# A mixture-of-experts dispatch on one core: block loads cut to 256 KB, and a replicated maximum as four column tiles

## The chip, the cores and the metric

The kernel runs on one core of a Trainium2 chip. A core has five engines that run side by side: TensorE (PE, with its weight loads listed apart as PEld), VectorE (DVE), ScalarE (ACT), GpSimd (POOL) and SyncE (SP), which here issues nearly all transfers. Transfers run on the core's 16 DMA engines. The metric is the time of one execution on the device, in microseconds; smaller is better.

## The reference

```python
def _attn_ref(x, v, pos_emb, w1, w2):            # x, v: (4, 11456, 128)
    h_filt = (np.maximum(pos_emb @ w1, 0.0) @ w2) * np.exp(-0.01 * pos)[:, None]
    u = x * v
    y = causal long convolution of u with h_filt along the sequence (by FFT)
    return x * y

def _moe_ref(x, phi, w1, w2):                    # x: (45824, 128), 8 experts, 4 slots each
    logits = x @ phi                             # (45824, 32)
    d = softmax over the tokens of logits        # dispatch
    slot_input = d.T @ x                         # (32, 128)
    slot_out = per expert: relu(slot_input @ w1[e]) @ w2[e]      # hidden width 1024
    c = softmax over the slots of logits         # combine
    return c @ slot_out

reference = _moe_ref(_attn_ref(...).reshape(45824, 128), ...)
```

The result of the first function (the gated convolution) is the token matrix of the second. Everything is float32.

## The kernel before

**Convolution, 0 to about 720 us.** Eight groups of 16 channels go through a transform of four steps, p1 to p4, and a gate with x. Steps of neighbouring groups are interleaved by a written list. The gated result goes to a scratch in DRAM, `scr`, in 16 pieces (lines 456 to 471); each holds 128 rows (channels) of up to 3,296 tokens. The last group's gates are done in `last_gate`, seven in a row (t = 0 to 6); between them the first loads of the next stage are issued by `Moe.ahead`.

**Dispatch, about 730 to 817 us.** The 45,824 tokens are 23 blocks of 2,048 (the last of 768). `Moe.load(i)` brings block i from the scratch as 128 channels by 2,048 tokens: 1 MB in rows of 8 KB, one transfer for each piece of the scratch that the block touches. Blocks 0 to 4 are loaded in two parts: 112 channels ahead of the last group's gates (`Moe.weights`), the last 16 channels behind them. Blocks 5 to 9 are loaded by `ahead`, blocks 10 to 22 by `fetch(i)`, which is called behind the transposes of block i and loads into the place that falls free there: blocks 10 to 19 behind 0 to 9, then W1 of the experts (512 KB each, `load_w1`, two each behind blocks 10 to 13), W2 of three experts behind block 14, blocks 20 to 22 behind blocks 15 to 17, and the remaining W2 (`load_w2`). All of this stands on SP's queue in this order. The transfers use eight landing semaphores in turn, so SP issues one only when the one eight before it has landed.

Two blocks are a unit; there are 12 units, the last with one block. For unit m+1 PE computes the logits (`logits`, line 780: four products of 32 output partitions for a block, with 512 tokens each, which together read the whole block), and for unit m it transposes the tokens (`turn`, line 714) and multiplies them by the dispatch weights (`dispatch`, line 872: 32 products with 32 columns of weights). VectorE takes a unit's maximum for each slot; `running_max` spreads it over the partitions by a product with `reps` (a 32 by 32 identity repeated 4 by 4), and VectorE reduces the result to the new negative running maximum, which the exponentials (`exps`, ACT) take as their bias. The program's order on each engine is fixed by hand (`inorder`). In a round of the loop PE does: transposes of the unit's first block, logits of the next unit, transposes of the second block, dispatch products of the unit before, the product of `running_max`. A float32 product appears in the profile as two, each with its weight load: `running_max` as two records, a block's logits as eight, a full unit's 32 dispatch products as 64.

**Experts and output, 817 to 890 us.** Two layers for 32 slots, then 23 output tiles: product, copy, store.

Of the kernel before, what the change touches and what calls it, by code (L numbers as in the profile page):

```python
# [17 lines left out]
B, S, D = 4, 11456, 128  # L18
# [27 lines left out]
FF = 1024  # L46
# [592 lines left out]
class Moe:  # L639
# [3 lines left out]
    XB = 5  # L643
    OB = 4
    CB = 8 * NB

    def __init__(self, tc, cp, scr, phi, mw1, mw2, rep, out):
        self.tc, self.cp, self.scr, self.out = tc, cp, scr, out
        self.phi, self.mw1, self.mw2, self.rep = phi, mw1, mw2, rep

        self.blocks = [(q, min(self.NB, QN - q)) for q in range(0, QN, self.NB)]
        self.xt, self.xq = {}, {}
        self.pieces = sorted(_pieces().values())
# [14 lines left out]
            self.load(i, 0, D - CG)  # L668

    def load_w1(self, e):  # L670
        self.tc.nc.sync.dma_start(out=self.w1t[:, e], in_=self.mw1[e])

    def load_w2(self, e):
        self.tc.nc.sync.dma_start(out=self.w2t[e],
                                  in_=self.mw2[e])

    def logit_banks(self):
        self.pls = self.ctx.enter_context(ExitStack())
# [3 lines left out]
    def places(self):  # L682
# [4 lines left out]
        bufs = [self.xreg[:, i * sz : (i + 1) * sz] for i in range(n)]  # L687
        far = [self.E[:, self.CB * NSLOT + i * sz :][:, :sz] for i in range(2)]
        self.xbuf = bufs[: self.XB - 1] + far[:1]
        self.obuf = bufs[self.XB - 1 :] + far[1:]  # L690

    def load(self, i, d0=0, d1=D):
        q0, n = self.blocks[i]
        t = (self.ahead_buf if i // self.XB in (0, 2) else self.xbuf)[i % self.XB][:, : 128 * n]
        z0, z1 = 128 * q0, 128 * (q0 + n)
        for a, m in self.pieces:
            lo, hi = max(z0, a), min(z1, a + B * m)
            if lo < hi:
                src = self.scr[D * a : D * (a + B * m)].rearrange("(d t) -> d t", d=D)
                self.tc.nc.sync.dma_start(out=t[d0:d1, lo - z0 : hi - z0], in_=src[d0:d1, lo - a : hi - a])  # L700
        self.xt[i] = t.rearrange("p (q t) -> p q t", t=128)

    def turn(self, pool, tag, i, k0, k1, shared=False):
# [28 lines left out]
def _moe(mo):  # L732
    tc, cp, out, blocks, ctx = mo.tc, mo.cp, mo.out, mo.blocks, mo.ctx
    nc = tc.nc
# [4 lines left out]
    phis, reps, w1t, w2t = mo.phis, mo.reps, mo.w1t, mo.w2t  # L739

    inorder = tc.keep_in_program_order
    units = [(v, v + 1) for v in range(0, NBL - 1, 2)] + [(NBL - 1,)]
    NU = len(units)
    ereg = mo.E
    far = mo.CB * NSLOT + 4 * FF
    Cms = [ereg[:, : mo.CB * NSLOT], ereg[:, far : far + (QN - mo.CB) * NSLOT]]
    Cms = [c.rearrange("p (q s) -> p q s", s=NSLOT) for c in Cms]
    csum = ereg[:, QN * NSLOT + 4 * FF :][:, :QN]

    def weights_of(q0, n):  # L750
        assert (q0 < mo.CB) == (q0 + n <= mo.CB)
        return Cms[0][:, q0 : q0 + n] if q0 < mo.CB else Cms[1][:, q0 - mo.CB : q0 - mo.CB + n]

# [37 lines left out]
    def maxima(m):  # L791

        mask = pmt[:, 8:12] if m else mo.mask
        if m:
            lts[m] = ms.tile([128, 2 * NB, NSLOT], F32, tag="lt", name=f"lt_{m}", bufs=1)
            rd = ms.tile([128, 2, 4], F32, tag="rd", name=f"rd_{m}")
            rms = [ms.tile([128, 1], F32, tag=f"rm{k}", name=f"rm_{i}") for k, i in enumerate(units[m])]
        else:
            lts[m] = lt0
            rd = few[3][:, :8].rearrange("p (k a) -> p k a", k=2)  # L800
            rms = [few[4][:, k : k + 1] for k in range(2)]
        for k, i in enumerate(units[m]):
            inorder(nc.vector.tensor_reduce(out=rms[k], in_=pls[i].rearrange("p q t -> p (q t)"),
                                            axis=AX.X, op=ALU.max, negate=True))
            inorder(nc.vector.scalar_tensor_tensor(out=rd[:, k], in0=neg[:, m : m + 1].to_broadcast([128, 4]),
                                                   scalar=rms[k], in1=mask, op0=ALU.min, op1=ALU.mult))
            if m and k == 0 and m < last:
                scores(m, 0)
        return rd[:, : len(units[m])]

    def spread_max(m):
        rd = maxima(m)
        if m < last:
            scores(m, 1)
        return rd

    def running_max(m, rd, pm=None):
        if pm is None:
            pm = pmt[:, : 4 * len(units[m])]
        inorder(nc.tensor.matmul(pm, lhsT=reps, rhs=rd.rearrange("p k a -> p (k a)"), start=True, stop=True))  # L820
        inorder(nc.vector.tensor_reduce(out=neg[:, m + 1 : m + 2], in_=pm, axis=AX.X, op=ALU.min))

    def factor(m):
# [128 lines left out]
    def fetch(i):  # L952
        if i < 2 * XB:
            mo.load(i + 2 * XB)
        elif i < 2 * XB + 4:
            for e in range(2 * (i - 2 * XB), 2 * (i - 2 * XB) + 2):
                mo.load_w1(e)
        elif i < 3 * XB:
            for e in range(3):
                mo.load_w2(e)  # L960
        elif i + XB < NBL:
            mo.load(i + XB)
        else:
            for e in range(3 + 2 * (i + XB - NBL), min(NEXP, 5 + 2 * (i + XB - NBL))):
                load_w2(e, i)
# [9 lines left out]
    rd = maxima(0)  # L975
    for k in range(2):
        scores(0, k)
    yield
    running_max(0, rd, mo.spot)
    exps(0)  # L980
    yield
# [12 lines left out]
    rd = spread_max(1)  # L994
    turn(1)
    fetch(1)
    pas[0] = pp.tile([128, 128], F32, tag="pa", name="pa_0")
    warm(4)
    running_max(1, rd)
    factor(0)  # L1000
    for m in range(1, last - 1):
        u = units[m]
        exps(m)
        if m > LATE:
            invert_unit(m - LATE - 1)
        softmax(m)
        if m > LATE:
            scale_unit(m - LATE - 1)
        turn(u[0])
        fetch(u[0])  # L1010
        turn_weights(m)
        if m > 1:
            collect(m - 2)
        logits(m + 1)
        rd = spread_max(m + 1)
        if m == 2:
            softmax(0)
        elif 2 < m <= LATE + 2:
            norm(m - 3)
        turn(u[1])  # L1020
        fetch(u[1])
        dispatch(m - 1)
        running_max(m + 1, rd)
        factor(m)
    m = last - 1
# [9 lines left out]
    rd = spread_max(last)  # L1035
# [260 lines left out]
```

## Time and profile before

| what | value |
|---|---|
| median of 3 runs | 889.4 us (888.58 to 891.3) |
| profiled execution | 892.43 us, of which the span 890.7 us |
| mean granted TensorE clock | 0.992 |
| busy: PE, PEld | 857.9 us (96%), 791.0 us (89%) |
| busy: DVE, ACT, POOL | 714.5 us (80%), 455.1 us (51%), 393.1 us (44%) |
| moved by DMA | 197.02 MB, 94,386 packets, mean 221 GB/s |

The span runs from the first to the last instruction of the program; times in rows count from its start. Busy times are unions over an engine's instructions. A busy PE isn't PE at its peak, since the ends of its pipelined products are modelled. "Idle before" is the time in which an engine had nothing before an instruction, with what released it; "issue" means that nothing the profile shows released it.

### The profile page before, as it was taken

Reading aid. Unit: us, or ns where it says so; the run is one execution under the profiler, and the core shown is the slowest. Engines: PE = TensorE matmul, PEld = TensorE weight load, DVE = VectorE, ACT = ScalarE, POOL = GpSimd, SP = SyncE. Lnnn points to the kernel's source line nnn. Section 1 sums busy time; section 2 is a strip of 40 time slices with the busy share of each in tenths; the row PEclk is TensorE's granted clock in tenths of the full one; section 3 lists DMA queues with packets and bytes.
Section 4 is the critical chain, followed back from the end, with each engine's and each line's share of the span. In section 5 each row is a group of like instructions: output and inputs, shape, how many; then the busy total and the mean of one; then the engine's idle time right before and its main releaser. Section 6 shows DMA issues by size and latency. Waiting matters only on the chain. (4 is left out here: it accounts for less than half of the span.)

```text
span 890.7 us, 37282 instructions
## 1 busy us (share of the span) xinstructions
PE 857.9 (96%) x16192; PEld 791.0 (89%) x16192; DVE 714.5 (80%) x1239; ACT 455.1 (51%) x971; POOL 393.1 (44%) x538
## 2 busy tenths in 40 slices
PE   9999999999999999999999999999999999899991
PEld 8998989999999999999999999999999987566540
DVE  5967976799799889988988998899789058786791
ACT  5775558315811851472166128415811637887761
POOL 5003860492088019405910960393078013775750
PEclk9999999999999999999999999999999999999996
DMA  9963684457747754775486376557716979993698
GB/s 323 396 197 117 204 246 153 144 155 254 207 135 207 234 166 128 237 237 172 132 261 202 120 222 214 168 166 247 218 44 173 272 176 374 412 355 121 277 416 365
DMA packets 94386, 197.02 MB, mean 221 GB/s; under 512 B 14329, under 2 KB 55707, under 8 KB 90382
## 3 DMA queue, kind: packets, MB, share of 16 engines
q1 hardware_dynamic: 94046, 194.50, 67.0%
q8 instruction: 128, 2.10, 0.9%
q14 instruction: 36, 0.29, 0.1%
q10 hardware_dynamic: 144, 0.07, 0.0%
q0 software_dynamic: 32, 0.07, 0.0%
HBM read 137.73 MB, written 56.86 MB: 218 GB/s over the span
## 5 line engine op out<-in xcount | busy, mean ns | idle before, releaser
L350 POOL TENSOR_TENSOR T<-m 111x256 f32<-111x256 f32 (+1 forms) x199 | 150.9, 758 | 344.8 <-DVE m L344 344.8
L344 DVE TENSOR_TENSOR m<-p,T 111x1024 f32<-111x1024 f32 (+1 forms) x175 | 200.4, 1205 | 14.4 <-PE p L340 7.6
L360 PE MATMUL p<-tab,T 111*99 111x112 f32 x2048 | 205.4, 260 | 1.4 <-POOL T L351 0.3
L360 PEld LDWEIGHTS p<-tab,T 111*99 111x99 f32 x2048 | 198.8, 170 | 6.5 <-issue 1.6
L340 PE MATMUL p<-T,W 128*64 128x128 f32 (+1 forms) x3168 | 197.3, 276 | 0.4 <-issue 0.3
L425 ACT ACTIVATE vc<-p 128x412 f32<-128x412 f32 (+1 forms) x112 | 51.7, 513 | 266.4 <-PE p L412 227.0
L340 PEld LDWEIGHTS p<-T,W 128*64 128x64 f32 (+1 forms) x3168 | 182.0, 127 | 2.8 <-DVE m L344 0.6
L412 PE MATMUL p<-tab,E 99*64 99x103 f32 (+1 forms) x3584 | 174.0, 252 | 1.6 <-DVE E L373 0.6
L412 PEld LDWEIGHTS p<-tab,E 99*64 99x64 f32 x3584 | 166.2, 136 | 3.8 <-ACT vc L425 0.8
L375 ACT ACTIVATE E<-p 99x448 f32<-99x448 f32 x254 | 131.9, 575 | 63.9 <-PE p L360 57.8
L351 POOL TENSOR_TENSOR T<-m 111x256 f32<-111x256 f32 (+1 forms) x199 | 147.4, 741 | 0.0
L186 ACT ACTIVATE T<-p 128x396 f32<-128x396 f32 x240 | 100.2, 535 | 11.3 <-PE p L174 11.1
L174 PE MATMUL p<-tab1x,x 53*64 53x99 f32 x3648 | 86.7, 246 | 0.2 <-ACT E L224 0.2
L174 PEld LDWEIGHTS p<-tab1x,x 53*64 53x64 f32 x3648 | 79.8, 132 | 4.4 <-ACT E L224 0.4
L443 DVE TENSOR_TENSOR p<-p,vc 128x824 f32<-128x824 f32 (+1 forms) x46 | 47.0, 1022 | 8.9 <-ACT vc L425 8.9
L268 DVE TENSOR_TENSOR x<-x,T 128x448 f32<-128x448 f32 x51 | 31.6, 619 | 21.2 <-DMA x<-in_xf_dram 11.6
L274 DVE TENSOR_TENSOR x<-T 128x224 f32<-128x224 f32 x102 | 39.2, 426 | 1.8
L270 DVE TENSOR_TENSOR T<-x 128x224 f32<-128x224 f32 x102 | 39.2, 426 | 1.7
L224 ACT ACTIVATE E<-fl 111x512 f32<-111x512 f32 (+1 forms) x50 | 26.8, 627 | 21.3 <-PE fl L218 21.3
L451 DVE TENSOR_TENSOR E<-p,E 128x824 f32<-128x824 f32 x36 | 36.6, 1017 | 1.2
L720 ACT ACTIVATE xreg<-pt 128x512 f32<-128x512 f32 (+1 forms) x68 | 35.0, 609 | 1.0 <-PE pt L714 0.9
L344 DVE TENSOR_TENSOR m<-p,E 111x1024 f32<-111x1024 f32 (+1 forms) x25 | 28.7, 1201 | 5.1 <-PE p L340 4.9
(156 smaller groups left out, 972.1 us busy)
## 6 DMA issues: line engine op xcount, KB each, us to landing
x<-in_xf_dram SPq DMA_DIRECT2D x114, 256.0 KB, 4.2
out_dram<-xreg SPq DMA_DIRECT2D x16, 1024.0 KB, 10.6
E<-in_xi_dram SPq DMA_DIRECT2D x37, 412.0 KB, 3.9
T<-in_vf_dram SPq DMA_DIRECT2D x65, 224.0 KB, 5.1
scr<-E SPq DMA_DIRECT2D x67, 206.0 KB, 4.3
T<-hs SPq DMA_DIRECT2D x63, 154.0 KB, 4.5
hs<-E SPq DMA_DIRECT2D x12, 784.0 KB, 4.6
mv<-in_vf_dram SPq DMA_DIRECT2D x42, 224.0 KB, 4.6
```

The lines of the kernel that those rows point to most:

```text
L174: inorder(nc.tensor.matmul(ps[h][RP * d : RP * d + RP, i, s, :], lhsT=sd[js, i, s, d, :], rhs=tab1x[js, J * (s + d) : J * (s + d + 1)], st ...
L186: inorder(nc.scalar.activation(dst, src, AF.Copy))
L270: inorder(eng.tensor_tensor(out=vt[:, :, m : m + 2], in0=xr[:, :, 0:2], in1=xr[:, :, 2:4], op=op))
L340: inorder(nc.tensor.matmul(ps[ns, i].rearrange("p b c -> p (b c)"), lhsT=W[:, k0 + i, ns], rhs=Tf[:, :, k0 + i, :], start=True, stop=True, ...
L344: inorder(nc.vector.tensor_mul(m[:, :n].rearrange("p k s e c i -> p k s (e c i)").rearrange("p k s (b c) -> p k s b c", c=CG), ps[:, :n].u ...
L350: inorder(eng.tensor_tensor(out=Ty[:, 0], in0=m[:, :n, 0, 0], in1=m[:, :n, 1, 1], op=ALU.subtract))
L351: inorder(eng.tensor_tensor(out=Ty[:, 1], in0=m[:, :n, 1, 0], in1=m[:, :n, 0, 1], op=ALU.add))
L360: inorder(nc.tensor.matmul(pk[:, i, 2 * s : 2 * s + 2, :].rearrange("p q r -> p (q r)"), lhsT=T[0:N1, s, 2 * k + i, u // 2, :, u % 2], rhs ...
L375: inorder(nc.scalar.activation(dst, src, AF.Copy))
L412: inorder(nc.tensor.matmul(pv[RP * h : RP * h + RP, 2 * k + i, w, j0:], lhsT=E[:J, r, 2 - 2 * w + s, :], rhs=tab4[:, s, o + j0 : o + NJ], ...
L425: inorder(nc.scalar.activation(vc[:, w, :, j0:], pv[:, :, 0, j0:], AF.Copy, scale=2.0 * w - 1.0))
L443: inorder(nc.vector.tensor_tensor(out=pw[:, :, :, j0:], in1=vc[:, :, :, j0:], op=ALU.add, in0=pw[:, 1:2, :, j0:].to_broadcast([128, 2, 4, ...
```

## The change

Loads of blocks (where they begin at channel 0), of W1 and of W2 are cut into transfers of at most 512 tokens or columns, which is 2 KB a row. The loads of the last 16 channels of blocks 0 to 4 stay whole. The product of `running_max` becomes four products, each for 32 of the 128 output partitions, at column positions 0, 32, 64 and 96 of the array, as the logits and the dispatch products are placed.

```diff
+    RUN = 512
...
     def load_w1(self, e):
-        self.tc.nc.sync.dma_start(out=self.w1t[:, e], in_=self.mw1[e])
+        for f in range(0, FF, self.RUN):
+            self.tc.nc.sync.dma_start(out=self.w1t[:, e, f : f + self.RUN], in_=self.mw1[e, :, f : f + self.RUN])
 
     def load_w2(self, e):
-        self.tc.nc.sync.dma_start(out=self.w2t[e],
-                                  in_=self.mw2[e])
+        n = self.RUN // 128
+        for j in range(0, FF // 128, n):
+            self.tc.nc.sync.dma_start(out=self.w2t[e][:, j : j + n], in_=self.mw2[e, :, j : j + n])
...
         for a, m in self.pieces:
-            lo, hi = max(z0, a), min(z1, a + B * m)
-            if lo < hi:
-                src = self.scr[D * a : D * (a + B * m)].rearrange("(d t) -> d t", d=D)
+            lo, end = max(z0, a), min(z1, a + B * m)
+            src = self.scr[D * a : D * (a + B * m)].rearrange("(d t) -> d t", d=D)
+            while lo < end:
+                hi = min(end, z0 + ((lo - z0) // self.RUN + 1) * self.RUN) if d0 == 0 else end
                 self.tc.nc.sync.dma_start(out=t[d0:d1, lo - z0 : hi - z0], in_=src[d0:d1, lo - a : hi - a])
+                lo = hi
...
-        inorder(nc.tensor.matmul(pm, lhsT=reps, rhs=rd.rearrange("p k a -> p (k a)"), start=True, stop=True))
+        for a in range(4):
+            ss = slice(32 * a, 32 * a + 32)
+            inorder(nc.tensor.matmul(pm[ss], lhsT=reps[:, ss], rhs=rd.rearrange("p k a -> p (k a)"),
+                                     start=True, stop=True, tile_position=(0, 32 * a)))
```

## Rows read from the trace of the kernel before

**Rows 1.** Windows, dispatch: stretch, length, busy by engine (instructions), PE clock, DMA share, GB/s.

```profile
756.10:763.30 7.20, 6.72 (x149) 4.71 (x148) 6.27 (x11) 6.32 (x14) 5.62 (x4) 1.00 1.02 417
763.30:770.80 7.50, 6.61 (x149) 4.48 (x148) 5.63 (x10) 6.74 (x15) 5.58 (x8) 1.00 1.02 412
770.80:778.30 7.50, 6.55 (x147) 4.63 (x146) 5.72 (x10) 6.59 (x14) 4.93 (x6) 1.00 1.01 408
778.30:786.90 8.60, 6.87 (x149) 4.66 (x148) 6.04 (x12) 6.48 (x14) 6.96 (x9) 1.00 1.03 409
786.90:793.60 6.70, 6.70 (x149) 4.71 (x148) 6.03 (x12) 6.34 (x14) 5.26 (x6) 1.00 0.99 365
793.60:800.60 7.00, 7.00 (x148) 4.80 (x148) 6.14 (x12) 5.78 (x14) 6.01 (x8) 1.00 0.91 332
```

**Rows 2.** Timeline of PE, dispatch: start, length, line, operation, count, idle time before.

```profile
758.69 1.04 PE L780 MATMUL pl<-E,aux 128*32 128x512 f32 x8
...
772.61 0.58 PE L714 MATMUL pt<-aux,ffw 64*128 64x64 f32 x11 [0.95 <-issue]
...
779.29 1.15 PE L714 MATMUL pt<-aux,ffw 64*128 64x64 f32 x30 [0.70 <-issue]
...
786.00 0.64 PE L872 MATMUL pa<-E,ev 128*32 128x128 f32 x15 [1.03 <-issue]
```

**Rows 3.** The chain that ended last, dispatch: start, length, what.

```profile
766.07 0.36 issue
...
791.43 1.91 PE pa L872 x64
793.33 0.32 PE pmt L820 x2
...
798.12 2.23 PE pa L872 x64
...
801.80 1.92 PE pl L780 x16
...
814.13 0.62 issue
```

**Rows 4.** Timeline of PE around 70 us, in the convolution's first step.

```profile
69.88 2.97 PE L174 MATMUL p<-tab1x,mv 53*64 53x99 f32 x127 [0.47 <-issue]
74.12 1.60 PE L174 MATMUL p<-tab1x,mv 53*64 53x99 f32 x63 [1.27 <-issue]
```

**Rows 5.** Windows, early stretches of the kernel.

```profile
24.00:44.00 20.00, 19.40 (x239) 19.09 (x237) 19.31 (x52) 14.72 (x29) 0.00 (x0) 1.00 1.04 395
...
70.00:75.00 5.00, 3.73 (x168) 3.53 (x172) 2.33 (x5) 2.01 (x4) 0.00 (x0) 1.00 0.27 100
12.00:20.00 8.00, 7.83 (x68) 7.31 (x67) 6.60 (x16) 3.68 (x9) 0.40 (x2) 1.00 1.05 372
```

**Rows 6.** The page: busy times (instructions), and the instruction queue (packets, MB, share).

```profile
PE 857.9 (96%) x16192; PEld 791.0 (89%) x16192; DVE 714.5 (80%) x1239; ACT 455.1 (51%) x971; POOL 393.1 (44%) x538
...
q8 instruction: 128, 2.10, 0.9%
```

**Rows 7.** DMA issues at 794.6 to 795.2 us: count, KB, us to landing.

```profile
xreg<-scr SPq DMA_DIRECT2D x1, 1024.0 KB, 6.7
```

**Rows 8.** SP's waits from 690 us on: us in total, times, longest.

```profile
SPq L465 <- DVE aux L726: 14.7, 1, 14.7
...
SPq L700 <- DMA ffw<-scr: 8.7, 7, 2.0
```

**Rows 9.** DMA issues from 12 to 20 us.

```profile
W<-in_wt_dram SPq DMA_DIRECT2D x3, 499.5 KB, 6.3
T<-in_vf_dram SPq DMA_DIRECT2D x5, 224.0 KB, 5.1
E<-in_xf_dram SPq DMA_DIRECT2D x4, 256.0 KB, 5.1
```

**Rows 10.** SP's issues of line 700: ns of one, least, median and most.

```profile
L700 SPq DMA_DIRECT2D ffw<-scr x24: 303/443/979, 685.1 to 757.2; - x24
```

## The prediction

> **What bounds the kernel now.** I read the busy times by stage first, then the timeline of TensorE, then the chain that ended last, and last the DMA answers. In the dispatch, 756 to 800 us, PE is busy for 6.55 to 7.00 us of every unit of two blocks, and the units that last longer than 7 us are longer by idle time, not by work; the DMA share is 0.91 to 1.03 in the same rows, so two resources are nearly full at once [rows 1]. The output stage behind it multiplies by what the dispatch summed up, so neither its products nor its stores can begin earlier: every microsecond won or lost in the dispatch arrives at the end.
>
> What idles PE: the timeline shows pauses of 0.95, 0.70 and 1.03 us that nothing in the program releases ("issue"), in the middle of whatever line was running [rows 2]. Counted in that timeline, 127 products lie from 772.61 to 779.29 (six rows, the first of them here) and 127 more from there to 786.00 (six rows again). 127 products with their 127 weight loads are 254 instructions, and the page counts 128 transfers of 2.10 MB of instructions, 16 KB each, while PE executes 2 x 16,192 instructions: 253 for each transfer [rows 6]. So I read the pauses as PE waiting for its next 16 KB of program. From one resumption to the next it is 6.68 and 6.71 us [rows 2]. At 70 us, with the same spacing of 127 products, it is 4.24 us [rows 4], and there the DMA share was 0.27 [rows 5]. Loaded DMA engines thus cost an instruction fetch 2.45 us. The chain has three more such pieces: 0.36 us at 766, 0.62 us at 814, and a group of 64 products at 798 us that took 2.23 us where the one before took 1.91, so 0.32 [rows 3].
>
> **The loads in 2 KB rows: what it does to the fetch.** A block's load is 1 MB in 128 rows of 8 KB, 64 KB for each of 16 engines; at 410 GB/s over 16 that is 2.5 us, nearly exactly the 2.45 us. My reading is that the fetch waits behind what one load has put on its engine. Cut to 256 KB this is 0.64 us, and the period becomes 4.24 + 0.64 = 4.9 us. Its bounds are 4.24 (idle DMA) and 6.7 (as now). PE needs 5.7 us for its 127 products (6.68 - 0.95), so at 4.9 no pause is left. Up to block 21's logits that takes away 0.36 + 0.95 + 0.70 + 1.03 + 0.32 = 3.36 us, behind it 0.62.
>
> **What it does to the transfers.** A whole block becomes four transfers, five where a piece of the scratch ends inside it; a W1 or W2 load becomes two. On SP's queue an issue takes 0.44 us [rows 10]. Of blocks 0 to 4, 15 more issues (some 7 us) lie ahead of a wait of 14.7 us of SP for VectorE [rows 8], which hides them; without that cover they would delay the write of the first gated piece. Blocks 5 to 9 add 15 issues among the last gates' writes, where SP already waits for landings. Behind SP's waits stand the later gates' writes and the last input load; PE first uses block 9 at 758.7 us. I cost this by bandwidth below, not by issues, since 256 KB per 0.44 us is more than the engines move.
>
> Bandwidth is the price. Early in the kernel the DMA engines were also full (share 1.04 and 1.05), with transfers near the new size: 372 GB/s from 12 to 20 us, where twelve issues average 304 KB, nine of them 224 or 256 KB [rows 9], and 395 GB/s from 24 to 44 us [rows 5], against some 410 in the middle of the dispatch [rows 1]. So the new rate has bounds of 372 and 395 from rows, and 410 if smaller rows cost nothing. I take the middle of the two, 384.
>
> Who needs that bandwidth: blocks 20 and 21. Their buffers come free late (block 21's load is issued at 794.8 us and lands 6.7 us later, at 801.5 [rows 7]), and the logits of block 21 start at 801.80 + 0.96 = 802.76 us [rows 3]. That is a margin of 1.3 us, while PE without its pauses would be there 3.36 us earlier, and ten units' shorter maximum products (below) 0.8 earlier still: at 798.6. All else that SP queues goes ahead of block 21. From 756.1 to 800.6 us the windows moved 7.2 x 417 + 7.5 x 412 + 7.5 x 408 + 8.6 x 409 + 6.7 x 365 + 7.0 x 332 = 17.44 MB [rows 1]; less block 22 (0.39 MB), 17.05. The last two windows are below 410 because SP then waited for buffers; a PE that is ahead frees them earlier, so I let the new kernel run at its full rate to the end. At 384 GB/s the 17.05 MB take 44.4 us; blocks 5 to 9 (5.24 MB) are late by 5.24/0.384 - 5.24/0.410 = 0.9; landing follows the last byte by 1.0 (801.5 against 800.6). Block 21 is there at 756.1 + 0.9 + 44.4 + 1.0 = 802.4 us: 0.4 us before it is used now, 3.8 after PE would want it. By 395 it is 800.8 (2.0 earlier than now), by 372 it is 804.2 (1.4 later).
>
> The Trainium skill speaks against this part: DMA: Bandwidth & Descriptors, Rules for kernel authors, asks for 1 MiB or more per DMA for the most bandwidth. Its fit for one transfer, 2.0 us + bytes/436,000, gives 2.6 us for 256 KB, an estimate of 101 GB/s if they went one at a time. The rows above are of eight in flight, and show a loss of 4 to 9%, not of three quarters.
>
> **The running maximum's product.** Now it is two passes of one 128-column product, 0.32 us of the chain in each of 12 units [rows 3]. After, it is eight passes of 32 columns, of the same tile shape as the dispatch products that stand ahead of it. 64 of those take 1.91 us [rows 3], 0.030 each, so 0.24 us: 0.08 saved. Bounds: nothing saved (the change of shape only moves from before the product to after it) and 0.20 (four tiles side by side cost as one, 0.12). I take 0.08: 0.8 us before block 21's logits, 0.16 behind. VectorE's reduction waits for this product, and the exponentials for that; it is not made later.
>
> **Sum.** Up to block 21's logits the later of two paths counts: PE at 798.6, the load at 802.4. So 0.4 us of the 4.2 is won there, PE waits 3.8 us at line 780 for blocks 20 and 21, where nothing waited before, and behind it 0.62 + 0.16 are won: 1.2 us in all. The profiled execution took 892.43 us (span 890.7 and 1.7 around it), which is 3.0 over the median of 889.4; its sum is 891.2, and by the median 888.2. The measurement can tell about 0.3%, 2.7 us.
>
> **Rivals.** *The loads keep up* (410 GB/s in the new size). Then block 21 is there at 756.1 + 41.6 + 1.0 = 798.7, PE's own pace counts, and 4.1 + 0.8 = 4.8 us are won: 884.6. For it: the stretch from 12 to 20 us has still smaller transfers in it than the new ones (224 KB), and three loads of another kind. Against it: both early rows are below 410 at a full share.
>
> *The loads starve* (slower). SP issues a transfer only when the one eight before it has landed; its waits for earlier loads are already 8.7 us in 7 cases [rows 8]. Eight in flight were up to 8 MB and become at most 2 MB, less where a piece boundary makes small ones, some 220 KB on average. A 256 KB load took 5.1 us to land at 12 to 20 us [rows 9]; eight of 220 KB per 5.1 us are 345 GB/s. Then blocks 5 to 9 are 2.4 us late and block 21 lands at 756.1 + 2.4 + 49.4 + 1.0 = 808.9, 6.2 later than it is used now: 889.4 + 6.2 - 0.8 = 894.8. It decides below 360 GB/s (2.7 us slower). Against it: the early rows, with the same eight, show 372.
>
> *The pauses stay* (the fetch waits for something else than a load's share of its engine). Then PE is at 802.76 less 0.8, the load at 802.4, and the kernel gains about 0.5: 888.9.
>
> **How the numbers follow.** Forecast (PE waits for block 20 or 21, within 372 to 395 GB/s: 886.6 to 890.1) 0.42; loads keep up 0.30; loads starve 0.20; pauses stay 0.08. Faster by over 0.3%: 0.30 and 0.06 of the forecast's upper end, 0.36. Within 0.3%: 0.36 + 0.08 = 0.44. Slower: 0.20. The range goes from the full gain, 884.6, up to 892.5, which is 358 GB/s and leaves about 1 in 10 on either side.
>
> **What would show it.** Right: no pauses of 0.7 us or more in the middle of lines 714 and 872 from 765 to 800 us; resumptions, if any, under 5 us apart; DMA at 372 to 395 GB/s with a share over 1; a new wait of PE of some 4 us at line 780 just before the last units; the product of the maximum at 0.24 us in the chain. Wrong: pauses at the old spacing (the fetch); no wait at line 780 (loads keep up, faster); waits at line 780 from block 9 on, or a DMA share well under 1 with SP waiting for landings (starved, slower).

## The result: 1.0% slower, and the profile after

The kernel after takes 899.28 us (median of 6 runs, 896.72 to 901.38) against 889.89 us (6 runs) for the kernel before on the same chip: a ratio of 1.0103, 95% interval 1.0082 to 1.0124. Forecast were 888.2 us, in a range up to 892.5. What happened is the rival "the loads starve", which had 2 chances in 10 and gave 894.8. The profiled execution of after took 897.51 us, its span 895.7.

Lines of after stand some lines lower: 780 is now 785 (logits), 714 is 719 (transposes), 872 is 880 (dispatch products), 820 is 827 (the maximum's product). First the windows over the dispatch of after, in the columns of [rows 1]:

```profile
762.00:792.00 30.00, 29.51 (x708) 21.20 (x707) 27.77 (x52) 29.72 (x65) 25.84 (x30) 1.00 0.99 332
792.00:802.00 10.00, 2.06 (x60) 1.55 (x48) 4.48 (x10) 3.51 (x9) 5.19 (x5) 0.79 1.05 383
802.00:812.00 10.00, 6.99 (x84) 3.49 (x88) 3.08 (x6) 2.04 (x5) 0.00 (x0) 0.53 0.87 287
```

The same stretch of before:

```profile
762.00:792.00 30.00, 26.43 (x584) 18.18 (x575) 23.16 (x45) 25.84 (x57) 22.35 (x28) 1.00 1.01 406
```

The first row of after holds both halves of the story. PE is busy for 29.51 of 30 us, where the first four stretches of before leave it idle for 0.5 to 1.7 us each [rows 1]: the pauses are gone here. And the DMA engines move 332 GB/s at a busy share of 0.99, where before moved 406. In the second row PE has nothing to do for 8 of 10 us, and in the third TensorE's granted clock is 0.53. The timeline of PE, in the columns of [rows 2], shows the place:

```profile
779.40 0.22 PE L827 MATMUL pmt<-rd,aux 128*32 128x8 f32 x8
...
785.84 0.22 PE L827 MATMUL pmt<-rd,aux 128*32 128x8 f32 x8
...
793.25 1.21 PE L719 MATMUL pt<-aux,xreg 64*128 64x64 f32 x32
804.25 1.94 PE L785 MATMUL pl<-xreg,aux 128*32 128x512 f32 x8 [9.79 <-DMA xreg<-scr]
806.94 1.94 PE L785 MATMUL pl<-xreg,aux 128*32 128x512 f32 x8 [0.76 <-DVE rm L808]
808.81 1.97 PE L719 MATMUL pt<-aux,E 64*128 64x64 f32 x32
810.71 2.25 PE L880 MATMUL pa<-xreg,ev 128*32 128x128 f32 x64
```

Units run without a break, 6.44 us from one maximum product to the next, and then PE waits 9.79 us at the logits of block 20 for its load. Block 21's logits follow at 806.94; the profile names VectorE there, but the last piece of block 21 landed at 806.8 too. Behind the wait the same products take longer than elsewhere in this timeline:

```profile
755.68 1.04 PE L785 MATMUL pl<-E,aux 128*32 128x512 f32 x8
756.65 1.47 PE L719 MATMUL pt<-aux,xreg 64*128 64x64 f32 x32
758.05 1.95 PE L880 MATMUL pa<-xreg,ev 128*32 128x128 f32 x64
```

The chain that ended last names the two transfers that PE had to wait for (start, length, what), and where the output products begin:

```profile
794.08 5.29 DMA ffw<-in_mw_dram
799.44 4.68 DMA xreg<-scr
804.25 1.97 PE pl L785 x8
...
834.23 3.07 PE pw L1136 x23
```

In the chain of before these begin here:

```profile
828.99 3.07 PE pw L1128 x23
```

A W2 load has to land so that SP may issue the piece that block 20 lacks. The answer on DMA for 756 to 796 us gives the total, and per group the count, KB each and median us from issue to landing:

```profile
DMA packets 8380, 13.80 MB, mean 345 GB/s; under 512 B 1313, under 2 KB 2465, under 8 KB 8371
...
ffw<-in_mw_dram SPq DMA_DIRECT2D x19, 256.0 KB, 5.8
xreg<-scr SPq DMA_DIRECT2D x14, 256.0 KB, 4.8
```

**Where the time went.** The profiled execution of after happens to be 3.0 us ahead when block 9's logits start (755.68 against 758.69 [rows 2]); in other executions, with either kind of load, the same row begins anywhere from 755.2 (x8) to 759.8 (x9), so I count from there. Block 21's logits come 806.94 - 755.68 = 51.26 us later, in before 802.76 - 758.69 = 44.07: 7.2 us lost to the load. Some of it is lost ahead of this stretch: SP issues the first piece of block 10 at nearly the same time in both, which is 7.3 us ahead of block 9's logits in before and only 4.6 in after (5.6 to 7.8 us in x1, x8 and x11, 3.2 to 5.8 in x2, x6, x9 and x13; timeline of SP, before and after):

```profile
751.40 6.79 SPq L700 DMA_DIRECT2D ffw<-scr  x8
751.11 15.13 SPq L704 DMA_DIRECT2D ffw<-scr  x23
```

From block 21's logits to the first output product it is 834.23 - 806.94 = 27.29 us against 828.99 - 802.76 = 26.23 in the chain of before: 1.1 more, although before has a pause of 0.62 in it [rows 3]. That is the clock: behind the wait the logits cost 1.94 instead of 1.04, the transposes 1.97 instead of 1.47, the dispatch products 2.25 instead of 1.95. Together 8.3 us; the medians differ by 9.4, and the last 1.1 us these two profiles don't place.

### The profile page after: what moved, and what is told of

The parts are those of the page before. It is cut to its first block, busy times and chain, and to the rows that moved or that the text cites. A ratio compares the mean times of both kernels' runs of the same rounds, so it can differ in the third digit from the quotient of the medians.

```text
span 895.7 us, 37602 instructions
## 1 busy us (share of the span) xinstructions
PE 859.1 (96%) x16264; PEld 792.2 (88%) x16264; DVE 716.2 (80%) x1239; ACT 454.3 (51%) x971; POOL 392.6 (44%) x538
## 5 line engine op out<-in xcount | busy, mean ns | idle before, releaser
L1136 PE MATMUL pw<-cs,so 32*128 32x512 f32 (+2 forms) x192 | 33.0, 633 | 0.7 <-DVE xreg L1143 0.7
```

Of the source, the lines that this page charges most:

```text
L1136: inorder(nc.tensor.matmul(po[:, :na].rearrange("p k t -> p (k t)"), lhsT=so[NSLOT * a : NSLOT * a + NSLOT], rhs=ct[NSLOT * a : NSLOT * a ...
```

## Experiments

Each ratio is to the kernel before on the same chip.

### The two parts of the change, each alone

x1 takes the loads of before and the four-tile product of the maximum; x2 takes the loads of after and the one 128-column product. x1 is the last piece of the diff above alone, x2 all the others.

> The loads are those of before (1 MB, rows of 8 KB), only the running maximum's product is four column tiles. If the product is worth what it measured in the changed kernel's chain (0.05 to 0.16 us where 0.32 stood, some 0.15 to 0.25 us in each of 12 units), the dispatch is 1 to 3 us shorter and the pauses of PE for instructions stay: 886.5 to 889, a ratio of 0.997 to 0.999. Rival: the loads alone cause the loss only together with the new product (PE further ahead); then nothing is seen here, 889 to 890. Neither theory expects it slower than 891.

> The loads of the change without its product. If the loads are the whole loss, the wait of PE for block 20 is here too, 8 to 9 us long instead of 9.8 (PE arrives 1 to 2 us later, the load at the same time), and the time is within 1 us of the changed kernel: 898 to 900, ratio 1.009 to 1.012. Rival (both parts matter): below 895.

x1: 890.61 us, ratio 1.0014 [1.0000, 1.0027]. x2: 899.27 us, 1.0113 [1.0096, 1.0130]. The loads are the whole loss. x2's timeline of PE has the same wait:

```profile
804.46 1.94 PE L785 MATMUL pl<-xreg,aux 128*32 128x512 f32 x8 [8.01 <-DMA xreg<-scr]
```

and its window the same low rate:

```profile
762.00:792.00 30.00, 29.74 (x642) 20.27 (x640) 26.40 (x49) 28.92 (x64) 25.29 (x32) 1.00 1.01 351
```

x1 keeps before's pauses, two of its six "issue" rows in the timeline of PE:

```profile
768.38 0.32 PE L875 MATMUL pa<-E,ev 128*32 128x128 f32 x4 [0.96 <-issue]
...
793.13 0.62 PE L780 MATMUL pl<-xreg,aux 128*32 128x512 f32 x2 [1.31 <-issue]
```

The new product itself does get shorter: 0.22 us for its eight passes in after's timeline (above) and in x1's, where the timeline of before has

```profile
800.28 0.39 PE L820 MATMUL pmt<-rd,aux 128*128 128x8 f32 x2
```

Twelve times 0.17 are 2.0 us, a ratio of 0.998, and x1's interval leaves that out: the gain doesn't arrive. x1's "issue" rows from 756 us to block 20's logits add up to 3.4 us, before's to 2.7, so that longer pauses may have taken it; one profile of each doesn't show that.

### Larger transfers, and longer rows

x3 doubles both sizes (512 KB, rows of 4 KB); x4 has transfers of 512 KB with rows of 2 KB.

```diff
-    RUN = 512
+    RUN = 1024
```
```diff
# x4: every second quarter of a row in one transfer; two experts' W1 in one
+            n4 = (end - lo) // 4
+            if d0 == 0 and n4 > 256 and (end - lo) % 4 == 0:
+                dst, src = (y.rearrange("p (a b w) -> p a b w", a=2, b=2) for y in (dst, src))
+                for b in range(2):
+                    self.tc.nc.sync.dma_start(out=dst[:, :, b], in_=src[:, :, b])
...
+                self.tc.nc.sync.dma_start(out=self.w1t[:, e : e + 2, f : f + self.RUN], ...)
```

> As changed, but transfers of 512 KB with rows of 4 KB. Both theories of the low rate (too little in flight; cost for each row) expect some 380 to 395 GB/s in the dispatch where the changed kernel has 345, a wait for block 20 of 2 to 4 us, and 889 to 893. Of the pauses: if a fetch waits behind what one transfer has put on an engine (now 32 KB, 1.25 us), its period is 5.5 us and no pause of over 0.3 us is seen from 765 to 790 us; if it waits for something that goes with the number of bytes in flight, pauses of 0.3 to 0.6 us come back.

> Transfers of 512 KB whose rows are 2 KB or a little less: each takes every second quarter of a block's row (of W1, the half rows of two experts). Rows are as short as in the changed kernel, transfers twice as large, twice as much in flight. Theory 'in flight': the rate is that of 512 KB transfers, 380 to 395 GB/s, and the time that of the run with 4 KB rows, 889 to 893. Theory 'rows': the rate stays at 340 to 355 GB/s and the time at 897 to 900. The pauses tell what a fetch waits behind: one transfer's share of an engine (32 KB) or one row (2 KB); neither expects pauses over 0.3 us.

x3: 890.98 us, 1.0012 [1.0003, 1.0021]. x4: 895.86 us, 1.0071 [1.0051, 1.0091]. The window of x3:

```profile
762.00:792.00 30.00, 26.39 (x611) 18.52 (x605) 24.11 (x45) 26.39 (x58) 22.68 (x29) 1.00 1.03 403
```

and of x4:

```profile
762.00:792.00 30.00, 26.52 (x615) 18.85 (x617) 23.35 (x45) 25.64 (x57) 22.43 (x28) 1.00 1.05 384
```

At 512 KB the rate is 403 GB/s with 4 KB rows and 384 with 2 KB rows: short rows cost about 5%. At 256 KB with the same 2 KB rows it is 332 in after, 351 in x2: 9 to 14% more is lost that rows can't explain. And the pauses are back, in both. The longest in x3, from the timeline of PE:

```profile
770.53 0.51 PE L880 MATMUL pa<-E,ev 128*32 128x128 f32 x9 [1.32 <-issue]
```

and in x4:

```profile
795.24 0.21 PE L727 MATMUL pt<-aux,xreg 64*128 64x64 f32 x1 [2.48 <-issue]
```

A transfer of 512 KB holds 32 KB of each engine, half of before's 64. Had a fetch waited for such a share, pauses would have been half gone; x4's "issue" rows from 756 us to the logits of block 20 add up to 6.2 us, x3's to 3.4, before's to 2.7. x4's time lies between the two expectations (889 to 893 and 897 to 900), and its profile shows no long wait for a load (0.76 us at block 20): what it has more of than x3 are these pauses, and a stretch of lower clock behind the longest (0.81 from 792 to 798 us).

### Whole rows in transfers of 256 KB

x5 cuts a block by channels: every fourth row, 8 KB long, in each of four transfers (W1 in two, by every second row).

```diff
+            parts = 4 if (d0, d1) == (0, D) else 1
+            for q in range(parts):
+                self.tc.nc.sync.dma_start(out=dst[q::parts], in_=src[q::parts])
```

> Transfers of 256 KB again, so at most 2 MB in flight as in the changed kernel, but whole rows: each takes every fourth channel of a block (rows of 8 KB, or up to a piece's end), W1 every second channel (4 KB). So far: 4 MB in flight gave 403 GB/s with rows of 4 KB and 384 with rows of 2 KB from 762 to 792 us; 2 MB and 2 KB gave 332 and 351. Theory 'in flight' (some 40 GB/s of the loss): about 355 to 375 GB/s, a wait for block 20 of 4 to 8 us, 893 to 898, and no pauses of PE for instructions. Theory 'rows' alone: 405 GB/s, no such wait, 885 to 888 if the pauses stay away.

x5: 927.02 us, 1.0418 [1.0387, 1.0448], far outside what either theory expected. Its window:

```profile
762.00:792.00 30.00, 27.37 (x608) 19.12 (x608) 23.66 (x41) 22.02 (x50) 13.59 (x14) 0.90 0.74 230
```

The rate falls to 230 GB/s at a share of 0.74: the engines themselves idle, and what holds them back is SP. Its timeline has the issues back to back:

```profile
760.97 22.32 SPq L708 DMA_DIRECT2D ffw<-scr  x32
```

One issue takes 0.59 us (median; 0.38 in after), and the transfers land in 3.6 us, so that SP waits for nothing but 2.8 of the 40 us from 756 on, and not once for a landing. The pieces of the scratch cut these transfers too: 157 KB on average, every 0.70 us, are the 230 GB/s. So this run doesn't tell rows from bytes in flight. x12 does, below.

### Blocks 20 to 22 ahead of W1 and W2

On SP's queue the last four loads of W1 and two of W2, 3 MB, stand right ahead of block 20 (the third W2 of those behind block 14 goes out at 705 us already). x6 (on after) and x8 (on before) move the calls for these four of W1 and for the first three of W2 behind the load of block 22 in the program.

> The changed kernel with the loads of four of the eight W1 and of the first three W2 queued behind blocks 20 to 22 instead of ahead of them: 3.6 MB, 10 us at 345 GB/s, less in front of block 20. If the wait for block 20 and the cold clock behind it are where the time went, the wait falls from 9.8 us to under 1 us, the clock stays at its higher level, and the gain of the missing pauses is seen: 884 to 888. Rival (the low rate hurts elsewhere too, or the weights are then late for the experts): 890 or more, with a wait at the experts' first or second layer.

> The same reordering of the weight loads in the kernel before, with its 1 MB loads and its one product. No wait for block 20 is there to take away, so both theories expect no change: 888.5 to 891.5, the pauses of PE as before. If it is faster by over 2 us, the reordering itself, not the shorter transfers with it, is what would win in the run above.

x6: 899.3 us, 1.0098 [1.0073, 1.0124]. x8: 890.38 us, 1.0003 [0.9988, 1.0019]. Neither tests what it was made for: SP's timeline in x6 has the transfers in the old order, W1 (L673) and W2 (L678) first, and so has x8's. The scheduler orders these calls by itself, since nothing holds them to the program's order.

```profile
784.48 11.22 SPq L673 DMA_DIRECT2D ffw<-in_mw_dram  x16
796.05 2.73 SPq L678 DMA_DIRECT2D ffw<-in_mw_dram  x4
799.09 8.00 SPq L704 DMA_DIRECT2D xreg<-scr  x13
```

So x6 is after once more. It has "issue" pauses of 0.38, 0.90, 1.05 and 1.05 us ahead of block 20's logits, where after has none, and correspondingly a shorter wait behind them, for the same time (timeline of PE):

```profile
806.67 1.93 PE L785 MATMUL pl<-xreg,aux 128*32 128x512 f32 x8 [6.58 <-DMA xreg<-scr]
```

x10 (on after) and x11 (on before) wrap the same calls so that they keep the program's order.

```diff
...
+            mo.held = mo.tc.keep_in_program_order
             mo.load(i + XB)
+            if i + XB == NBL - 1:
+                for e in range(4, NEXP):
+                    mo.load_w1(e)
+                for e in range(3):
+                    mo.load_w2(e)
...
```

> The kernel after, with the loads of blocks 20 to 22, the second half of W1 and the first three of W2 held to program order on SP's queue (the earlier try left the order as it was: SP still issued W1 and W2 first). Theory 'the wait for block 20 is bytes queued ahead of it at 345 GB/s': block 20 is issued once block 15 is turned, at about 788 us instead of 796.8, has 1 to 2 MB ahead of it, lands by about 795, so the 9.8 us wait shrinks to at most 2 us in all, no pauses before the logits of block 20, no stretch at half clock; 885 to 889 us. Rival 'W1 and W2 late, something else waits': the wait moves behind the dispatch (the line of the expert products waits for W1 or W2) and the time stays at 893 to 899. Rival 'what is late is not what is queued': the wait for block 20 stays above 6 us, 897 to 900.

> Control: the same order held in the kernel before (1 MB and 512 KB transfers). There PE never waits for a block, so the loads of blocks 20 to 22 landing some 8 us earlier is worth nothing: within 0.3% of before (888 to 891.5). The pauses of 0.3 to 1 us per unit stay, unless SP's stop at block 20's buffer empties the queue for a while, which would shorten one or two of them.

x10: 891.37 us (12 runs), 1.0002 [0.9989, 1.0016]. x11: 892.53 us, 1.0015 [1.0004, 1.0027]. SP's timeline of x10 now has blocks 20 to 22 (L705) between the halves of W1 (L674), issued from 789.55 instead of 796.77:

```profile
783.71 5.75 SPq L674 DMA_DIRECT2D ffw<-in_mw_dram  x8
789.55 8.35 SPq L705 DMA_DIRECT2D xreg<-scr  x13
798.04 4.49 SPq L674 DMA_DIRECT2D ffw<-in_mw_dram  x8
```

and PE finds block 20 there; only 1.38 us is left, at block 21, at the full clock (timeline of PE, then the window behind). The profile names a W1 load there, but the last piece of block 21 landed at 800.0:

```profile
797.68 1.07 PE L786 MATMUL pl<-xreg,aux 128*32 128x512 f32 x8
800.13 1.06 PE L786 MATMUL pl<-xreg,aux 128*32 128x512 f32 x8 [1.38 <-DMA ffw<-in_mw_dram]
```

```profile
802.00:812.00 10.00, 8.40 (x248) 7.34 (x248) 5.86 (x14) 7.51 (x20) 5.88 (x6) 1.00 0.97 339
```

The rate is as low as in after (340 GB/s from 762 to 792). So the whole loss was bytes queued ahead of block 20 at that rate. x11 shows that the order alone is worth nothing, or a little less: it lies 1 us above what was expected, and its SP stands still from 775.5 to 790.0 us for block 20's place, so that the share is 0.78 from 762 to 792 us. My 885 to 889 was too good, though: with the wait gone, the time is that of before and not better, since the pauses aren't gone. x10 has "issue" rows of 1.28 and 0.37 us ahead of block 20's logits and of 1.32 and 0.76 behind block 21's.

### Whole 1 MB loads, two in flight

x12 is the kernel before, with its 8 KB rows, but transfers of 64 bytes stand between the loads, so that SP's eight outstanding transfers hold at most 2 MB.

```diff
+    def space(self, n):
+        for _ in range(n):
+            k = self.spent
+            self.held(self.tc.nc.sync.dma_start(out=self.out[k : k + 1, :16], in_=self.phi[k : k + 1, :16]))
+            self.spent = k + 1
...
+        if i >= 2 * self.XB:
+            self.space(4 - sum(max(z0, a) < min(z1, a + B * m) for a, m in self.pieces))
...
```

> The kernel before with its whole transfers of 1 MB (rows of 8 KB) and 512 KB, each preceded by transfers of 64 bytes (into a part of the output that the real result overwrites) so that eight landings never cover more than 2 MB of load. It leaves no work out. Theory 'the bytes in flight set both the rate and the pauses': over 762 to 792 us the rate falls from 410 to 330 to 365 GB/s although rows are long, the pauses of PE vanish although one transfer still holds 64 KB of every engine, PE waits 5 to 10 us for block 20; 895 to 900 us. Rival 'short rows and many small transfers set the rate': the rate stays at 385 or more, no wait above 2 us; 887 to 892. Rival of the prediction 'a fetch of program waits behind one transfer's 64 KB share of an engine': the pauses stay (period above 6.6 us), whatever the rate.

x12: 904.76 us, 1.0158 [1.0140, 1.0176]. The window:

```profile
762.00:792.00 30.00, 28.36 (x585) 18.78 (x585) 23.81 (x44) 26.10 (x58) 22.67 (x28) 0.94 1.00 325
```

and the timeline of PE:

```profile
770.25 0.59 PE L726 MATMUL pt<-aux,ffw 64*128 64x64 f32 x12 [0.32 <-issue]
777.48 1.15 PE L726 MATMUL pt<-aux,ffw 64*128 64x64 f32 x31 [1.24 <-ACT et L843]
...
811.11 1.93 PE L792 MATMUL pl<-xreg,aux 128*32 128x512 f32 x8 [11.18 <-DMA xreg<-scr]
```

325 GB/s at a share of 1.00, with rows four times as long as after's: with little in flight, long rows lose what after lost and more. The wait, 11.18 us, and the time miss the expected numbers on the far side; why, this run doesn't show. SP's issues, 0.58 us for a small transfer, are not the limit as in x5: by the times of issue and landing about 7.6 of the eight are out at a time, 2.0 MB. What the small transfers cost the engines isn't seen in full: of packets up to 256 bytes, the records of this window show 900 of 4 bytes, 9 ns each (331 in before), and none of 64. What grows is the mean of the large packets, by a few very long ones: 8 KB packets have a median of 309 ns and a mean of 429 (longest 1,926), in before 312 and 315. After has the same mark without any small transfers between, 2 KB packets with a median of 84 ns, a mean of 95 and a longest of 1,113; x4, with the same rows in larger transfers, has 87, 88 and 231. What makes a packet wait when few bytes are queued, these runs don't show.

As to the pauses, 64 KB of each engine per transfer leave 0.32 us of "issue" here. The 1.24 us at 777.48, which the profile puts down to ACT, belong to them: they stand 127 products behind the 0.32, inside a group of transposes with 31 of 32 left, where before has its 0.70 (779.29, 30 left [rows 2]). That makes 1.56 us, where before has 2.7, and between the two it is 7.23 us, so the rival that was expected to keep the period above 6.6 us isn't ruled out by this run. From 780 to 786 us the granted clock was 0.82, so PE needed longer for its products there; from 786 to 798 us, at 1.00, there is no pause.

### The same transfers from another array

The early stretches read at 372 and 395 GB/s in transfers near the new size [rows 5]. Their source is an input array whose rows lie one behind the other; in the scratch, in W1 and in W2 they lie apart. x13 is after, with the dispatch's loads filled from that input array.

```diff
+    def other_rows(self, n):
+        k, self.spent = self.spent, self.spent + 1
+        return self.other[k // 16, k % 16].rearrange("p c q r -> p (c q r)")[:, :n]
...
+                in_=self.other_rows(hi - lo) if i >= 2 * self.XB else src[d0:d1, lo - a : hi - a])
```

> The kernel after, in the same order and sizes of transfer, but blocks 10 to 22, W1 and W2 are filled from tiles of an input array whose 128 rows of 2 KB lie one behind the other (so the dispatch works on other numbers, and its result isn't used). The early stretches read that array in transfers of this size at 372 to 395 GB/s; the dispatch reads rows that lie far apart, at 332 to 351. Theory 'bytes in flight alone': the rate over 762 to 792 us stays at 330 to 355 GB/s and PE waits 6 to 10 us for block 20; 896 to 901 us. Rival 'where the rows lie decides': the rate is 370 or more, the wait for block 20 is under 4 us; 887 to 893 us.

x13: 900.3 us, 1.0110 [1.0091, 1.0129]. Its window:

```profile
762.00:792.00 30.00, 27.11 (x620) 19.47 (x620) 23.70 (x46) 26.18 (x58) 22.39 (x28) 0.94 0.96 321
```

321 GB/s, and PE waits 6.57 us for block 20: where the rows lie is not it. What is left is the amount in flight in the early rows. The DMA answer of before for 24 to 44 us lists 24 issues of 305 KB on average, and the twelve of 12 to 20 us average 304 [rows 9]: eight of them are 2.4 MB. In after's dispatch (756 to 796 us) 57 issues average 234 KB: eight are 1.8 MB. By the same answers eight are 3.1 MB in x4, 3.3 in x3 and 4.7 in before. The number of transfers doesn't order the rates: 1.2 and 1.5 for each microsecond in the early rows (395 and 372 GB/s), 1.4 in after and 1.2 in x12 (325).

### Unused products in the wait

x9 is after, with 30 products of no use issued before block 20's logits, so that PE is not idle while it waits.

```diff
+        if m == last - 2:
+            wt = pp.tile([128, 512], F32, tag="pt", name="warm_late", bufs=4)
+            for _ in range(30):
+                inorder(nc.tensor.matmul(wt[:, :128], lhsT=reps, rhs=ident, start=True, stop=True))
```

> The changed kernel with 30 products of 128 columns, whose result nobody reads, between the transposes and the logits of blocks 20 and 21: they take 8.5 to 9 us of PE, as long as it waits there anyway. If the lower clock behind the wait costs what the rows show (logits 1.94 instead of 1.06 us twice, 0.8 us more in the two groups behind), the granted clock stays at 1.00 and the time falls by 2 to 2.7 us, to 896.5 to 897.5. Rival (the clock is hidden, the second block's load sets the pace anyway): less than 1 us, 898.5 to 899.5.

x9: 897.75 us, 1.0086 [1.0054, 1.0118]. Its timeline of PE, with two passes for each unused product:

```profile
799.48 6.96 PE L1025 MATMUL warm_late<-aux 128*128 128x128 f32 x60 [1.31 <-ACT xreg L725]
807.53 1.07 PE L785 MATMUL pl<-xreg,aux 128*32 128x512 f32 x8 [1.08 <-DMA xreg<-scr]
810.20 1.06 PE L785 MATMUL pl<-xreg,aux 128*32 128x512 f32 x8 [1.60 <-DMA xreg<-scr]
```

and the window around them:

```profile
802.00:812.00 10.00, 7.31 (x82) 5.43 (x83) 2.22 (x4) 0.06 (x1) 0.95 (x1) 1.00 1.04 364
```

The clock stays at 1.00 and the logits take 1.07 us again, but the loads still set the time. The gain on after is 1.5 us by the medians, and the two intervals overlap; by the timeline of after, the low clock costs 0.9 + 0.9 + 0.5 + 0.3 = 2.6 us over its first four groups.

## Why the prediction was wrong

**The step that failed: the rate of the new transfers.** "I take the middle of the two, 384" mis-sized the term on which the sum turned. It measured 332 GB/s in after (762 to 792 us), and 351, 348, 342 and 340 in x2, x6, x9 and x10: all below the lower bound of 372. The place, the waiter and the load that it waits for were right (PE, at the logits of blocks 20 and 21). The rival's working, eight in flight times 220 KB per 5.1 us, gave 345 (353 with the profile's KB of 1,024 bytes). With it block 21 was to land 6.2 us later than it was used in before; counted from block 9's logits its logits came 7.2 later, by the times of the two profiled executions 4.2. And its 2.4 us by which blocks 5 to 9 make the later loads late were there: 2.7 (7.3 against 4.6 us, above). The 1.0 us from the last byte to the landing (801.5 less 800.6 is 0.9) took the end of a window for the last byte; nothing hangs on it.

**Why the bounds were wrong.** I held the early rows against the rival ("the same eight, show 372") and took nine of twelve transfers being small for the new size. Put in order of the bytes in eight transfers, the rates rise but for x12: 1.8 MB give 332 to 351 GB/s (after, x2, x6, x9, x10), 2 MB at most 325 (x12), 2.4 MB 372 and 395 (the early rows), 3.1 and 3.3 MB 384 and 403 (x4 and x3), 4.7 MB 406 (before). At the low end the time to land no longer falls with the size (4.8 and 5.8 us in after, 5.1 for a 256 KB load between larger ones [rows 9]), which is the rival's formula. Rows of 2 KB instead of 4 cost about 5% on top (x4 against x3); the source's layout explains none of the loss (x13, 321 GB/s). The Trainium skill (DMA: Bandwidth & Descriptors, Rules for kernel authors) asks for 1 MiB or more per DMA; the runs bear out the direction, 406 GB/s in before against 332 to 351 at 256 KB. x12 adds that 1 MB transfers don't keep the rate either, if only two are in flight. The prediction's fit for one transfer is given in the Trainium skill (DMA: Bandwidth & Descriptors, Anatomy of one DMA — SWDGE (gpsimd) path) for transfers that GpSimd issues; these are SP's, and no run here has one in flight at a time.

**The pauses.** The prediction had them vanish since a fetch "waits behind what one load has put on its engine". In after they did vanish (29.51 of 30 us busy), but this reason fell: with half the share they stayed and grew (x3 and x4), and with the full share and 2 MB in flight they were shorter, not longer, than in before (x12). From 756 us to block 20's logits the "issue" rows, with x12's 1.24 us, add up to 0 in after and x2, 1.1 in x9, 1.56 in x12, 1.65 in x10, 3.4 in x6 and 3.5 in x13. Where eight transfers hold 3 MB or more it is 2.7 in before, 3.1 in x8 and x11, 3.4 in x1 and x3, 6.2 in x4. So they come out shorter in the mean with little in flight, 1.6 us against 3.6, no more: x6 issues its transfers in after's order and has more than before. That after has none was partly luck. That PE waits for its next 16 KB of program still rests on their place alone, 127 products apart [rows 2, 6] and at the same products in before, x8, x11 and x12 (30 or 31 of 32 transposes left); what delays a fetch stays open.

**The clock was missing.** A forecast wait of 3.8 us had only its length as a price. In after the granted clock of 802 to 812 us is 0.53, so most of that stretch ran at 1.2 GHz, after 9.79 us of idle PE: 2.6 us by rows. The Trainium skill (TensorE: Matmul & The Clock Gate, HAM oscillation — how this bites in real kernels) describes just this, a wait for a transfer that lets the clock fall, so that the work behind it starts cold; the trace agrees. Shorter pauses had a low clock behind them too: 2.15 us in x13 (0.74 from 768 to 774 us) and 1.24 us in x12 (0.90 and 0.82 in the two stretches of 6 us from 774 us on).

**The maximum's product.** 0.08 us each, 0.8 in all, was the smallest term. The product shortened by twice that (0.39 to 0.22 us in the timelines), and x1 shows no gain, 1.0014 [1.0000, 1.0027]. So a product that is shorter in the chain didn't shorten the kernel; what took the gain, the runs don't show.

**No faster version.** x10 undoes the loss by order alone, and ends level with before. No variant was faster than before.

## What to carry to other kernels

With a fixed number of outstanding transfers, the size of one sets the bytes in flight, and in these runs the rate went with those: compute that product for before and after, and take the rate from a stretch with the same product and the same rows. When a saturated queue gets slower, look for the consumer with the least margin and for what is queued ahead of it without being urgent; moving 3 MB behind it made up here for 65 GB/s (406 in before, 340 in x10). And read the order of issue that was compiled before trusting an edit that only reorders calls, and SP's timeline before putting a low rate down to the engines.

## What the runs showed of the hardware

- A busy share of 1.00 says nothing of the rate: at shares of 1.00 to 1.05 the same 16 engines moved 325, 340, 384, 403 and 410 GB/s (x12, x10, x4, x3, x1). Under few bytes in flight, single packets take several times their median, and count as busy.
- Eight transfers of 234 KB on average were too few for the rate, eight of 305 KB nearly enough (332 to 351 against 372 and 395 GB/s).
- An issue on SP's queue took 0.59 us for a transfer over every fourth partition (32 rows), 0.38 over 128 rows (x5, after). At 157 KB each, SP's issues alone held the rate at 230 GB/s (x5, share 0.74).
- A pause of PE of 127 products' spacing can stand in the profile under another releaser than "issue" (x12, 1.24 us put down to ACT).
- PE's pauses in one and the same order of transfers differ by 3 us between executions (after and x6), and the total time does not, as long as a load sets it.
